# Ten units' bonus products and a weight subtraction moved from GpSimd to VectorE, a weight addition and a range check moved in the order

## The chip, the cores and the metric

The kernel runs on one core of one Trainium2 chip. The metric is device time in microseconds (us). Engines are named as in the profile: PE (TensorE), PEld (its weight loads), DVE (VectorE), ACT (ScalarE), POOL (GpSimd), SP (SyncE, which issues the DMAs).

## The reference

Three stages follow each other, in float32. B, H, S, D = 4, 8, 768, 48; d_model 384; d_ff 1024; 4 experts of width 64.

```python
for t in range(S):                                     # 1: a linear recurrence, per batch and head
    cur = k_t (x) v_t                                  # outer product, D x D
    y_t = r_t @ (state + u * cur)
    state = w_t[:, None] * state + cur
h = relu(x @ w_in)                                     # 2: gated MLP with a convolution of 3 taps along S
c = conv3(h, conv_w)
x = (h * sigmoid(c)) @ w_out
out = sum over the 2 chosen of 4 experts of gate_e * (causal_softmax_attention_e(x) @ wo_e)   # 3
```

## The kernel before

Stages 1 and 2 run interleaved in `phase1`, in an order written out by hand for PE, DVE, ACT and POOL: what `slot(u)` calls, call by call, is what each engine does in that order. SP's DMAs are ordered by a scheduler. Stage 3 (class `Attention`) follows and is not touched.

Stage 1 is cut into 32 units (a batch, a half of the sequence, a pair of heads). `slot(u)` finishes unit u, prepares unit u+1 and does the output of unit u-1. For unit u+1 it runs, on DVE, `scan_d` (Dp, a running product, L205), `scan_f` (L210, Fp L212, K L215) and `queries` (Q, L220); on POOL `bonus` (L225, L226: r times k, times u, 128x288, in place); then `diag`: DVE sums the bonus to e (L231), and POOL spreads e onto a diagonal tile AT with two affine_selects (L234). For unit u it runs `check` (two ACT passes over w, L243, a range test that feeds a flag), and on PE `trans` (L266) and its ACT copy KT, `scores` (L252), `state` (L278); on DVE `carry` (L289 reads the state product from PSUM, L292 twice chains it over the chunks) and `masked` (L258, two copy_predicated that put the scores from PSUM into AT). For unit u-1, `yout` (PE L306, L312) and `rows` (ACT L324, DVE L325, a small POOL cast, and DMAs into X).

PSUM tiles of `trans`, `state` and `yout` come from one pool of two buffers ("m"), used in turn. So `trans(u+1)` takes the buffer that `state(u)` wrote, and waits until `carry(u)` has read it in L289.

Stage 2 starts in slot 5 with two groups a slot (`groups`): `mlp1` (PE L350, nine matmuls into hs, one PSUM buffer; ACT ht L354, ct L358), `conv` (DVE, two scalar_tensor_tensor, L369/L371 or L373/L374, then ACT tanh L377), `gate` (DVE L387), `mlp2` (PE L400, four groups later).

The weights w_in and w_out arrive as float64 in eight pieces of 768 numbers a partition and are turned to float32 by hand, two buffers each for the raw piece and the work tiles: `load_w` (DMA), `conv1_w` (ACT L72; DVE L75 and L76; POOL L77, an integer addition), and, for w_in alone, `conv2_w` (ACT L173 rounds to the high part, POOL L174 subtracts it for the low part). `check_w` (ACT L185, L186) tests a piece that is loaded a second time for values outside the range. The table `WS` says in which slot a piece is taken. `conv_w` converts the 24 convolution weights.

Of the kernel before, what the change touches and what calls it, by code (L numbers as in the profile page):

```python
# [16 lines left out]
OP = mybir.AluOpType  # L17
# [3 lines left out]
B, H, S, D = 4, 8, 768, 48  # L21
# [8 lines left out]
CH = NC // 2  # L30
# [10 lines left out]

X2_ON_DVE, V_ON_DVE, OUT_ON_DVE = (), (1,), (5,)
SCALED_ON_POOL = 13


def _f(ap):
    return ap.bitcast(F32)
# [40 lines left out]
def phase1(tc, nc, a, x2, ident, stat, lim, top, right, left2):  # L88
# [15 lines left out]
    T = {}  # L104
# [55 lines left out]
    def conv1_w(n, i):  # L160

        if wide:
            RW[n, i] = f64_fast(nc, raw, RW[n, i], WC, "w", None if n == "win" else wl(wout)[:, i * WC:(i + 1) * WC])

    def conv2_w(n, i):

        t = RW.pop((n, i))
        if n == "wout":
            if not wide:
                nc.scalar.activation(wl(wout)[:, i * WC:(i + 1) * WC], t, AF.Copy)  # L170
            return
        d0, d1 = (wl(d)[:, i * WC:(i + 1) * WC] for d in win)
        nc.scalar.activation(d0, t, AF.Copy)  # L173
        nc.gpsimd.tensor_tensor(d1, t, _f(d0), op=OP.subtract)  # L174

    RW = {}

    def check_w(n, i):

        if not wide:  # L180
            return
        t = RW.pop((n, i))
        o = 4 * NU + (i if n == "win" else 4 + i)
        hi = t.bitcast(F32).rearrange("p (n two) -> p n two", two=2)[:, :, 1]
        nc.scalar.activation(hi, hi, AF.Square)  # L185
        nc.scalar.activation(hi, hi, AF.Relu, bias=lim[:, 3:4], scale=-1.0, accum_out=stat[:, o:o + 1])  # L186
# [35 lines left out]
    def bonus(u):  # L222
        b, h, hp = split(u)
        m = T[u]["rn"]
        nc.gpsimd.tensor_tensor(m, m, T[u]["kn"], op=OP.mult)  # L225
        nc.gpsimd.tensor_tensor(m, m, u_b[:, hp][:, :, None].to_broadcast([128, 2, CH, D]), op=OP.mult)  # L226

    def diag(u):
        t = T[u]
        e = wk.tile([128, 2, CH], F32, name="e")  # L230
        nc.vector.tensor_reduce(e, t["rn"], axis=AX.X, op=OP.add)  # L231
        AT = t["AT"] = wk.tile([128, 2, CH, C], F32, name="AT")
        for j in range(2):
            nc.gpsimd.affine_select(AT[:, j], e[:, j][:, :, None].to_broadcast([128, CH, C]),  # L234
                                    pattern=[[0, CH], [1, C]], compare_op=OP.is_equal, fill=0.0, base=0,
                                    channel_multiplier=-1)

    def check(u):
        t = T[u]
        w, Fp = t["w"], t["Fp"]  # L240
        wc = w[:, 1:].rearrange("p (c t) -> p c t", c=CH)[:, :, 0:C]
        for z in range(2):
            nc.scalar.activation(Fp[:, :, 0:C], wc, AF.Relu, bias=lim[:, z:z + 1], scale=(-1.0, 1.0)[z],  # L243
                                 accum_out=stat[:, 2 * u + z:2 * u + z + 1])
# [135 lines left out]
    def gate(g):  # L380
        if not 0 <= g < NG:
            return
        h = g // NF % 2
        o, N = 2 * h, HT - 2 + 4 * h
        ht, st = G[g]
        gt = ml.tile([128, HT + 2], F32, name="gt", bufs=6)[:, 0:N]
        nc.vector.scalar_tensor_tensor(gt, st, 1.0, ht[:, o:o + N], op0=OP.add, op1=OP.mult)  # L387
        G[g] = gt
# [3 lines left out]
    def mlp2(g):  # L392
# [9 lines left out]
        if f == NF - 1:  # L402
# [11 lines left out]
    mine = mybir.EngineType  # L414
    mine = {mine.PE, mine.DVE, mine.Activation, mine.Pool}

    WS = ((2, "win", 0), (3, "win", 1), (4, "win", 2), (5, "wout", 0), (6, "win", 3), (7, "wout", 1), (8, "wout", 2),
          (9, "wout", 3)) + tuple((10 + i, ("win", "wout")[i % 2], i // 2) for i in range(8))

    def groups(g, last=False):  # L420
        if 0 <= g < NG:
            mlp1(g)
        if 0 <= g - LAG < NG:
            mlp2(g - LAG)

    def slot(u):

        ga = 2 * u - G0
        s1u, nxt = u < 2 * NU, u + 1 < 2 * NU
        for i, (z, n, m) in enumerate(WS):  # L430
            if u == z - 2:
                load_w(n, m)
        if s1u:
            trans(u)
        conv(ga - 1)
        if nxt:
            bonus(u + 1)
            scan_d(u + 1)
        for i, (z, n, m) in enumerate(WS[0:8]):
            if u == z:  # L440
                conv1_w(n, m)
        gate(ga - 1)
        groups(ga)
        if nxt:
            scan_f(u + 1)
        conv(ga)
        if nxt:
            queries(u + 1)
        gate(ga)
        if s1u:  # L450
            check(u)
            scores(u)
            state(u)
        if 0 < u <= 2 * NU:
            yout(u - 1)
        if nxt:
            diag(u + 1)
        if s1u:
            carry(u)
            masked(u)  # L460
        if 0 < u <= 2 * NU:
            rows(u - 1)
        for i, (z, n, m) in enumerate(WS):
            if u == z:
                (conv2_w if i < 8 else check_w)(n, m)
        if u == 1:
            conv_w()
        if u == 18:
            rawc.close()
        groups(ga + 1)  # L470
        if u + 3 < 2 * NU:
            load(u + 3)
# [646 lines left out]
```

## Time and profile before

| | |
|---|---|
| time, median of 3 runs | 658.96 us (657.47 to 659.04) |
| the profiled execution | 659.13 us, span of its trace 657.4 us |
| PE / DVE / ACT / POOL busy | 586.6 / 517.6 / 347.9 / 183.2 us |
| mean granted TensorE clock | 0.962 |

The span is the time from the first to the last instruction; the 1.7 us between it and the profiled execution's own time lie around it. Busy time is an average over stages; which engine sets the pace differs from stage to stage.

### The profile page before, as it was taken

Reading aid. Unit: us, or ns where it says so; the run is one execution under the profiler, and the core shown is the slowest. Engines: PE = TensorE matmul, PEld = TensorE weight load, DVE = VectorE, ACT = ScalarE, POOL = GpSimd, SP = SyncE. Lnnn points to the kernel's source line nnn. Section 1 sums busy time; section 2 is a strip of 40 time slices with the busy share of each in tenths; the row PEclk is TensorE's granted clock in tenths of the full one; section 3 lists DMA queues with packets and bytes.
Section 4 is the critical chain, followed back from the end, with each engine's and each line's share of the span. In section 5 each row is a group of like instructions: output and inputs, shape, how many; then the busy total and the mean of one; then the engine's idle time right before and its main releaser. Section 6 shows DMA issues by size and latency. Waiting matters only on the chain.

```text
span 657.4 us, 11247 instructions
## 1 busy us (share of the span) xinstructions
PE 586.6 (89%) x3978; PEld 464.9 (71%) x3978; DVE 517.6 (79%) x1151; ACT 347.9 (53%) x819; POOL 183.2 (28%) x245
## 2 busy tenths in 40 slices
PE   2665689799999999999999999989997999799896
PEld 1553567577676777777777776968786987788754
DVE  6999999988888999999995643688765876776471
ACT  3233444566666545556355552666654665556452
POOL 6478444222222233224321710030002002102260
PEclk9957789989999999999999999999998999999999
DMA  8655445475774455454513652265036514442502
GB/s 315 214 162 208 171 151 178 147 230 179 219 215 135 126 165 158 133 169 134 160 59 96 173 139 67 85 170 144 25 90 175 145 37 128 126 98 84 133 1 77
DMA packets 34401, 92.39 MB, mean 141 GB/s; under 512 B 5024, under 2 KB 14368, under 8 KB 34336
## 3 DMA queue, kind: packets, MB, share of 16 engines
q1 hardware_dynamic: 34336, 91.59, 46.7%
q8 instruction: 33, 0.54, 0.3%
q14 instruction: 32, 0.26, 0.1%
HBM read 53.77 MB, written 9.44 MB: 96 GB/s over the span
## 4 chain that ended last, share of the span: by engine, by line
PE 48%; DVE 29%; ACT 9%; DMA 7%; issue 4%; SPq 2%; POOL 1%; ACTq 0%; DVEq 0%; POOLq 0%
PE x L400 9%; PE hs L350 7%; PE m L767 6%; PE st L841 5%; PE m L891 5%; PE t L875 4%; DVE Fp L212 4%; PE m L903 4%; PE m L797 3%; DVE Dp L205 3%; DMA x<-x 2%; DVE AT L258 2%; DVE wm L76 2%; DVE ct L374 2%; DVE ct L369 2%
## 5 line engine op out<-in xcount | busy, mean ns | idle before, releaser
L400 PE MATMUL x<-gt,wout 128*128 128x386 f32 (+1 forms) x384 | 135.0, 490 | 0.0
L350 PE MATMUL hs<-X,win 128*128 128x384 f32 (+1 forms) x576 | 121.7, 357 | 8.2 <-ACT ht L354 8.1
L350 PEld LDWEIGHTS hs<-X,win 128*128 128x128 f32 x576 | 101.1, 193 | 17.6 <-ACT ht L354 11.7
L377 ACT ACTIVATE st<-ct 128x382 f32<-128x382 f32 (+1 forms) x64 | 33.6, 525 | 126.3 <-DVE ct L371 67.4
L400 PEld LDWEIGHTS x<-gt,wout 128*128 128x128 f32 x384 | 73.0, 192 | 35.8 <-issue 1.2
L855 ACT ACTIVATE A<-sm,mn 128x128 f32<-128x128 f32 (+5 forms) x96 | 63.8, 665 | 28.3 <-DVE mn L854 27.5
L854 DVE CUSTOM_DVE_ANT_0 sm<-st,mask 128x128 f32<-128x128 f32 (+5 forms) x96 | 58.3, 619 | 20.8 <-PE st L841 18.2
L234 POOL TENSOR_SCALAR_AFFINE_SELECT AT<-e 128x384 f32<-128x384 f32 x64 | 32.4, 531 | 141.8 <-DVE e L231 134.2
L875 PE MATMUL t<-ident,A 128*128 128x128 f32 x336 | 53.5, 276 | 2.1 <-ACT T L879 1.2
L266 PE MATMUL m<-ident,K 128*128 128x128 f32 x80 | 16.6, 312 | 36.6 <-DVE Ss L289 26.4
L841 PE MATMUL st<-sk,sq 128*128 128x384 f32 (+3 forms) x128 | 44.8, 360 | 2.7 <-DVE mn L854 1.8
L753 POOL TENSOR_TENSOR xs<-x,xs 128x768 fp32r<-128x768 f32 x12 | 22.4, 1884 | 88.8 <-ACT xs L752 88.8
L881 DVE COPY T<-t 128x128 f32<-128x128 f32 (+3 forms) x64 | 32.2, 504 | 18.4 <-PE t L875 17.9
L387 DVE SCALAR_TENSOR_TENSOR gt<-st,ht 128x382 f32<-128x382 f32 (+1 forms) x64 | 38.1, 596 | 10.9 <-ACT st L377 7.9
L841 PE MATMUL st<-sl,sq 128*128 128x384 f32 (+3 forms) x128 | 41.1, 334 | 5.8 <-DMA sl<-kl 5.8
L875 PEld LDWEIGHTS t<-ident,A 128*128 128x128 f32 x336 | 40.3, 140 | 8.4 <-issue 2.2
L252 PEld LDWEIGHTS sc<-Q,K 64*128 64x128 f32 x384 | 30.7, 218 | 20.5 <-issue 5.6
L266 PEld LDWEIGHTS m<-ident,K 128*128 128x128 f32 x80 | 11.0, 156 | 46.8 <-DVE Ss L289 29.8
L891 PE MATMUL m<-T,V 128*64 128x384 f32 (+2 forms) x288 | 43.8, 422 | 0.0
L879 ACT ACTIVATE T<-t 128x512 f32<-128x512 f32 (+3 forms) x64 | 28.6, 447 | 25.4 <-PE t L875 20.6
L252 PE MATMUL sc<-Q,K 64*128 64x128 f32 x384 | 37.6, 325 | 4.2 <-DVE AT L258 4.2
L358 ACT ACTIVATE ct<-ht,cwk 128x382 f32<-128x382 f32 (+1 forms) x64 | 39.5, 617 | 2.0
(126 smaller groups left out, 1216.2 us busy)
## 6 DMA issues: line engine op xcount, KB each, us to landing
wkr<-in_wkr SPq DMA_DIRECT2D x32, 578.0 KB, 3.8
rkv<-in_rkv SPq DMA_DIRECT2D x32, 480.0 KB, 4.5
rawt<-in_win SPq DMA_DIRECT2D x8, 768.0 KB, 5.5
rawt<-in_wout SPq DMA_DIRECT2D x8, 768.0 KB, 5.2
sk<-kh SPq DMA_DIRECT2D x32, 192.0 KB, 3.3
sl<-kl SPq DMA_DIRECT2D x32, 192.0 KB, 4.0
x<-x SPq DMA_DIRECT2D x12, 384.0 KB, 3.9
out_dram<-ot SPq DMA_DIRECT2D x24, 192.0 KB, 1.9
```

The lines of the kernel that those rows point to most:

```text
L252: nc.tensor.matmul(sc[j][:, c], t["K"][p, c], t["Q"][p, c], start=True, stop=True)
L350: nc.tensor.matmul(hs[:, 0:N], win[wi][:, f // 2, i, (f % 2) * 128:(f % 2 + 1) * 128], x[:, i, xi], start=(n == 0), stop=(n == 8))
L358: nc.scalar.activation(ct, ht[:, o:o + N], AF.Copy, scale=w[:, 1, f:f + 1])
L377: nc.scalar.activation(st, ct, AF.Tanh)
L387: nc.vector.scalar_tensor_tensor(gt, st, 1.0, ht[:, o:o + N], op0=OP.add, op1=OP.mult)
L400: nc.tensor.matmul(acc[0][i][:, 0:N], wout[:, f, i * 128:(i + 1) * 128], gt, start=(f == 0), stop=(f == NF - 1))
L767: nc.tensor.matmul(pt[:, 0:HT], w[wi][:, i, p * 128:(p + 1) * 128], xs[xi][:, i, s], start=(m == 0), stop=(m == 8))
L841: nc.tensor.matmul(st[:, z, 0:n], q[:, qi * C:(qi + 1) * C], k[:, z * n:(z + 1) * n], start=(i == 0), stop=(i == 1))
L854: nc.vector.tensor_tensor_reduce(o3, i3, m3, 1.0, 3e38, op0=OP.add, op1=OP.min, accum_out=mn)
L855: nc.scalar.activation(at, o3, AF.Exp, bias=mn, scale=-1.0, accum_out=rs[:, qi % 3:qi % 3 + 1])
L875: nc.tensor.transpose(pt[:, ki - k0], at[:, ki * C:(ki + 1) * C], self.ident)
L891: nc.tensor.matmul(po[o, lo:HT], V[:, ki, (2 * p + j) * 64:(2 * p + j + 1) * 64], Ts[j][:, ki, lo:], start=(ki == 0), stop=(ki == n - 1))
```

## The change

- `bonus` runs on DVE for units 0 to 9 and stays on POOL for the others. On DVE it is called right before `diag`, behind `yout` in the code, and no longer at the slot's start.
- `conv2_w`'s subtraction runs on DVE. It is now called early in the slot after the one in which the piece was added; `conv1_w` is now called late in the slot, between `diag` and `masked`, one slot number earlier.
- `masked` and `rows` now come ahead of `carry` on DVE.
- `check` is called ahead of `conv(ga)`, and `check_w` ahead of `scores`; in ACT's order the first is now ahead of the second tanh, the second ahead of `rows`' copy.
- `conv_w` moves from slot 1 to slot 0. The second loads for `check_w` are issued a slot later.

```diff
+BONUS_ON_DVE = 10
...
         d0, d1 = (wl(d)[:, i * WC:(i + 1) * WC] for d in win)
         nc.scalar.activation(d0, t, AF.Copy)
-        nc.gpsimd.tensor_tensor(d1, t, _f(d0), op=OP.subtract)
+        nc.vector.tensor_tensor(d1, t, _f(d0), op=OP.subtract)
...
         m = T[u]["rn"]
-        nc.gpsimd.tensor_tensor(m, m, T[u]["kn"], op=OP.mult)
-        nc.gpsimd.tensor_tensor(m, m, u_b[:, hp][:, :, None].to_broadcast([128, 2, CH, D]), op=OP.mult)
+        eng = nc.vector if u < BONUS_ON_DVE else nc.gpsimd
+        eng.tensor_tensor(m, m, T[u]["kn"], op=OP.mult)
+        eng.tensor_tensor(m, m, u_b[:, hp][:, :, None].to_broadcast([128, 2, CH, D]), op=OP.mult)
...
-    WS = ((2, "win", 0), (3, "win", 1), (4, "win", 2), (5, "wout", 0), (6, "win", 3), (7, "wout", 1), (8, "wout", 2),
-          (9, "wout", 3)) + tuple((10 + i, ("win", "wout")[i % 2], i // 2) for i in range(8))
+    WS = ((1, "win", 0), (2, "win", 1), (3, "win", 2), (4, "wout", 0), (5, "win", 3), (6, "wout", 1), (7, "wout", 2),
+          (8, "wout", 3))
+    WC2 = tuple((10 + i, ("win", "wout")[i % 2], i // 2) for i in range(8))
...
-            if u == z - 2:
+        for z, n, m in WS + WC2:
+            if u == z - 1:
                 load_w(n, m)
...
-            bonus(u + 1)
+            if u + 1 >= BONUS_ON_DVE:
+                bonus(u + 1)
             scan_d(u + 1)
-        for i, (z, n, m) in enumerate(WS[0:8]):
-            if u == z:
-                conv1_w(n, m)
+        for z, n, m in WS:
+            if u == z + 1:
+                conv2_w(n, m)
         gate(ga - 1)
         groups(ga)
+        if s1u:
+            check(u)
...
         gate(ga)
+        for z, n, m in WC2:
+            if u == z:
+                check_w(n, m)
         if s1u:
-            check(u)
             scores(u)
             state(u)
...
         if nxt:
+            if u + 1 < BONUS_ON_DVE:
+                bonus(u + 1)
             diag(u + 1)
+        for z, n, m in WS:
+            if u == z:
+                conv1_w(n, m)
         if s1u:
-            carry(u)
             masked(u)
         if 0 < u <= 2 * NU:
             rows(u - 1)
-        for i, (z, n, m) in enumerate(WS):
-            if u == z:
-                (conv2_w if i < 8 else check_w)(n, m)
-        if u == 1:
+        if s1u:
+            carry(u)
+        if u == 0:
             conv_w()
```

In the orders below the changed kernel's lines stand up to 11 numbers higher than those named so far. First, DVE at the program's start, before:

```order
L205 SCALAR_TENSOR_TENSOR Dp<-wkr,cD 128x387
L141 CAST msk<-Q 128x384
L210 RECIPROCAL cF<-Dp 128x3
L212 SCALAR_TENSOR_TENSOR Fp<-wkr,cF 128x387
L215 TENSOR_TENSOR K<-wkr,Fp 128x384
L220 TENSOR_TENSOR Q<-wkr,Dp 128x384
L231 TENSOR_REDUCE e<-rkv 128x6
```

and now:

```order
L142 CAST msk<-Q 128x384
L227 TENSOR_TENSOR rkv<-rkv 128x288
L228 TENSOR_TENSOR rkv<-rkv,u_b 128x288
L206 SCALAR_TENSOR_TENSOR Dp<-wkr,cD 128x387
L211 RECIPROCAL cF<-Dp 128x3
```

The first unit's bonus, which reads u_b, now stands ahead of the first scan. Second, DVE in slot 3 (unit 4 prepared, a piece of w_in in work as wm, Y of unit 2), before:

```order
L205 SCALAR_TENSOR_TENSOR Dp<-wkr,cD 128x387
L75 TENSOR_SCALAR wm<-rawt 128x768
L76 SCALAR_TENSOR_TENSOR wm<-rawt,wm 128x768
L210 RECIPROCAL cF<-Dp 128x3
L212 SCALAR_TENSOR_TENSOR Fp<-wkr,cF 128x387
L215 TENSOR_TENSOR K<-wkr,Fp 128x384
L220 TENSOR_TENSOR Q<-wkr,Dp 128x384
L231 TENSOR_REDUCE e<-rkv 128x6
L289 TENSOR_TENSOR Ss_128<-m,Dp 128x3x48
L292 SCALAR_TENSOR_TENSOR Ss_128<-Ss_128,Dp 128x48 x2
L258 COPY_PREDICATED AT<-msk,sc 128x384 x2
L325 TENSOR_TENSOR Y<-m,Y 128x384
```

and now, from Q on into the next slot's start:

```order
L221 TENSOR_TENSOR Q<-wkr,Dp 128x384
L227 TENSOR_TENSOR rkv<-rkv 128x288
L228 TENSOR_TENSOR rkv<-rkv,u_b 128x288
L233 TENSOR_REDUCE e<-rkv 128x6
L76 TENSOR_SCALAR wm<-rawt 128x768
L77 SCALAR_TENSOR_TENSOR wm<-rawt,wm 128x768
L260 COPY_PREDICATED AT<-msk,sc 128x384 x2
L327 TENSOR_TENSOR Y<-m,Y 128x384
L291 TENSOR_TENSOR Ss_128<-m,Dp 128x3x48
L294 SCALAR_TENSOR_TENSOR Ss_128<-Ss_128,Dp 128x48 x2
L206 SCALAR_TENSOR_TENSOR Dp<-wkr,cD 128x387
L175 TENSOR_TENSOR win_139<-wm,win_138 128x768
```

The two weight steps that POOL's addition (now L78) waits for stand ahead of the three operations that read PSUM (AT, Y, the first of Ss), and the reading of the state product (now L291) is the third of these. Third, ACT in slot 12, where a piece is checked (rawt), before:

```order
L377 ACTIVATE st<-ct 128x386
L354 ACTIVATE ht<-hs 128x388
L358 ACTIVATE ct<-ht,cwk 128x386
L377 ACTIVATE st<-ct 128x386
L243 ACTIVATE Fp,stat<-wkr,lim 128x3x128 x2
L324 ACTIVATE Y<-m 128x384
L185 ACTIVATE rawt<-rawt 128x768
L186 ACTIVATE rawt,stat<-rawt,lim 128x768
L354 ACTIVATE ht<-hs 128x388
```

and now:

```order
L379 ACTIVATE st<-ct 128x386
L356 ACTIVATE ht<-hs 128x388
L360 ACTIVATE ct<-ht,cwk 128x386
L245 ACTIVATE Fp,stat<-wkr,lim 128x3x128 x2
L379 ACTIVATE st<-ct 128x386
L186 ACTIVATE rawt<-rawt 128x768
L187 ACTIVATE rawt,stat<-rawt,lim 128x768
L326 ACTIVATE Y<-m 128x384
L356 ACTIVATE ht<-hs 128x388
```

The unit's check went ahead of the second tanh, and the piece's check from behind Y to ahead of it.

## Rows read from the trace of the kernel before

**Rows 1.** Stretches: from:to and length in us, busy us (x instructions) by engine, TensorE clock, DMA
```profile
25.33:122.27 96.94, 66.41 (x477) 51.34 (x476) 94.73 (x140) 39.03 (x85) 53.60 (x53) 0.79 0.55 179
122.27:211.71 89.44, 84.08 (x611) 63.30 (x610) 76.93 (x145) 58.42 (x126) 22.88 (x41) 0.98 0.64 193
211.71:334.63 122.92, 122.71 (x916) 93.35 (x915) 119.02 (x218) 64.88 (x153) 38.70 (x60) 1.00 0.46 143
```

**Rows 2.** Groups of instructions, DVE, 25.33 to 122.27: busy us, mean ns
```profile
L212 DVE TENSOR_TENSOR_SCAN Fp<-wkr,cF 128x387 f32<-128x387 f32 x8 | 14.6, 1822 | 0.3
L76 DVE SCALAR_TENSOR_TENSOR wm<-rawt,wm 128x768 int32<-128x768 int32 x8 | 12.2, 1519 | 0.3
L220 DVE TENSOR_TENSOR Q<-wkr,Dp 128x384 f32<-128x384 f32 x8 | 9.2, 1150 | 0.0
L215 DVE TENSOR_TENSOR K<-wkr,Fp 128x384 f32<-128x384 f32 x8 | 7.1, 890 | 0.3
L369 DVE SCALAR_TENSOR_TENSOR ct<-ht,cwk,ct 128x381 f32<-128x381 f32 x8 | 6.2, 769 | 0.0
```

**Rows 3.** Single lines, DVE, whole span: ns min/median/max, first and last start
```profile
L212 DVE TENSOR_TENSOR_SCAN Fp<-wkr,cF x32: 964/965/2412, 6.0 to 336.2; 128x387 f32<-128x387 f32 x32
L76 DVE SCALAR_TENSOR_TENSOR wm<-rawt,wm x8: 957/959/2458, 27.4 to 110.8; 128x768 int32<-128x768 int32 x8
L220 DVE TENSOR_TENSOR Q<-wkr,Dp x32: 546/553/2153, 8.0 to 338.8; 128x384 f32<-128x384 f32 x32
L215 DVE TENSOR_TENSOR K<-wkr,Fp x32: 557/559/1977, 7.5 to 337.2; 128x384 f32<-128x384 f32 x32
L369 DVE SCALAR_TENSOR_TENSOR ct<-ht,cwk,ct x32: 600/616/1269, 68.5 to 364.4; 128x381 f32<-128x381 f32 x32
L205 DVE TENSOR_TENSOR_SCAN Dp<-wkr,cD x32: 946/958/1568, 4.7 to 334.6; 128x387 f32<-128x387 f32 x32
L75 DVE TENSOR_SCALAR wm<-rawt x8: 527/529/535, 26.8 to 110.3; 128x768 int32<-128x768 int32 x8
L292 DVE SCALAR_TENSOR_TENSOR Ss<-Ss,Dp x64: 269/436/456, 14.9 to 348.7; 128x48 f32<-128x48 f32 x64
```

**Rows 4.** Timeline, DVE and POOL, slot 3: start us, us, instruction
```profile
41.00 2.15 DVE L220 TENSOR_TENSOR Q<-wkr,Dp 128x384 f32<-128x384 f32 x1
...
40.62 2.11 POOL L77 TENSOR_TENSOR wm<-wm,wy 128x768 int32<-128x768 int32 x1
```

**Rows 5.** Timeline, POOL, slot 22
```profile
259.92 0.80 POOL L225 TENSOR_TENSOR rkv<-rkv 128x288 f32<-128x288 f32 x1
260.80 0.81 POOL L226 TENSOR_TENSOR rkv<-rkv,u_b 128x288 f32<-128x288 f32 x1
```

**Rows 6.** Timeline, DVE, slot 22
```profile
258.67 0.25 DVE L289 TENSOR_TENSOR Ss<-m,Dp 128x96 f32<-128x96 f32 x1
...
259.80 1.06 DVE L258 COPY_PREDICATED AT<-msk,sc 128x384 f32<-128x384 uint32 x2
260.75 0.54 DVE L325 TENSOR_TENSOR Y<-m,Y 128x384 fp32r<-128x384 f32 x1
```

**Rows 7.** Timeline, the start, POOL and DVE; in brackets the idle time ahead
```profile
8.37 0.79 POOL L226 TENSOR_TENSOR rkv<-rkv,u_b 128x288 f32<-128x288 f32 x1 [1.74 <-DMA u_b<-in_u]
...
9.20 0.45 DVE L231 TENSOR_REDUCE e<-rkv 128x6 f32<-128x288 f32 x1 [0.69 <-POOL rkv L226]
```

**Rows 8.** Timeline, ACT, slot 17, in which a piece is checked
```profile
206.58 0.47 ACT L324 ACTIVATE Y<-m 128x384 fp32r<-128x384 f32 x1
206.95 0.91 ACT L185 ACTIVATE rawt<-rawt 128x768 f32<-128x768 f32 x1
...
208.90 0.47 ACT L354 ACTIVATE ht<-hs 128x388 f32<-128x388 f32 x1
```

**Rows 9.** Who waited for whom, 122.27 to 211.71: us in total, times, longest
```profile
DVE ct L369 <- ACT ct L358: 4.9, 4, 1.2
```

**Rows 10.** Timeline, PE, slot 22
```profile
260.36 0.38 PE L266 MATMUL m<-ident,K 128*128 128x128 f32 x2
```

More of the change, by code (lines that the diff above doesn't have):

```diff
@@ L462, in slot @@
             rows(u - 1)
-        for i, (z, n, m) in enumerate(WS):
-            if u == z:
-                (conv2_w if i < 8 else check_w)(n, m)
-        if u == 1:
+        if s1u:
+            carry(u)
+        if u == 0:
             conv_w()
```

## The prediction

> **What bounds the kernel now.** I read the busy time by stretches first, cutting stages 1 and 2 at the starts of the Dp scans, since one Dp runs in each slot. Three regimes show [rows 1]. From 25.33 to 122.27 us (slots 2 to 9) DVE is busy 94.73 of 96.94 us and PE 66.41: DVE sets the pace. From 211.71 to 334.63 (slots 18 to 29) PE is busy 122.71 of 122.92, so a slot lasts 122.92 / 12 = 10.24 us whatever DVE does. Between them (slots 10 to 17, those in which a weight piece is checked) PE is busy 84.08 of 89.44 us, so 5.36 us is the most that can be had there. After 334.63 nothing in the change matters but its shift in time.
>
> Next I asked what DVE's busy time is made of. The reader should set the mean of a line in slots 2 to 9 [rows 2] against its median over the span [rows 3]: the scan Fp takes 1.822 us where 0.965 is usual, L76 1.519 for 0.959, Q 1.150 for 0.553, K 0.890 for 0.559, the first convolution operation 0.769 for 0.616. Nothing in these operations changed; they are held. The timeline says by whom: Q starts at 41.00 and needs 2.15 us, while POOL's 768-wide addition runs from 40.62 to 42.73 [rows 4]; Q ends 0.42 us after it. So DVE operations with two SBUF inputs wait for POOL, and count as busy. This is also what tells which operations are immune: in slot 22 POOL's two products run from 259.92 to 261.61 [rows 5], and copy_predicated twice in 1.06 us and Y in 0.54 us, which read PSUM, are not stretched beside them [rows 6].
>
> **Slots 2 to 9, what goes.** Per line, eight times the difference: Fp 6.9, L76 4.5, Q 4.8, K 2.6, the convolution 1.2; Dp reaches 1.568 instead of 0.958 [rows 3] in two of these slots, 1.2 more. Sum 21.2 us of holding by the bonus products, the weight additions and the subtractions. The two carry operations of a slot take 0.436 each by the median and 0.269 at best [rows 3], since POOL's affine_selects run beside them; in the new order those run beside other work: 16 x 0.167 = 2.7 us. One slot's weight steps, 0.53 + 0.96 = 1.5 us, leave for slot 1. Together 25.4 us go.
>
> **Slots 2 to 9, what comes.** Four subtractions of 768 elements on DVE: no row has one there, L76 has the same two-input shape, 0.96 each, 3.8 us. Seven units' bonus on DVE, two products of 288 elements: between the 288-element sum of 0.45 [rows 7] and the 384-element product of 0.55 [rows 3], so 0.47, nearest the first; 14 x 0.47 = 6.6 us (bounds 6.3 to 7.7). And a new holding. The addition now starts behind L76 and takes 2.1 us [rows 4]; DVE has copy_predicated (0.95 from start to start), Y (0.46) and the first carry operation (0.3) to run beside it [rows 6], 1.7 us, and then the two carry operations have to wait. Ahead of that, L76 meets the affine_selects. Bounds for one slot: 0.45 us (2.1 less 1.7, and nothing for the affine_selects) to 2.1 us (the whole addition, no cover at all). I take 1.0, near the lower end, because rows 5 and 6 show the cover at work: 0.4 for L76 (two of the 0.167 above, rounded up) and 0.6 for the carry, the addition starting some 0.2 us late behind the second affine_select. Seven slots: 7.0 us. Together 17.4 come. Net: **-8.0 us**.
>
> [...]
>
> **The start and slots 0 and 1.** DVE now begins with the first unit's bonus, whose second product waits for u_b: POOL started it at 8.37 us after waiting 1.74 for that DMA [rows 7]. Dp, Fp, K and Q of the first unit, done before e at 9.20 until now [rows 7], queue behind it: 8.37 + 0.47 + 0.96 + 0.2 + 0.97 + 0.56 + 0.55, less 0.3 for the overlap of neighbours, gives e at about 11.8: +2.6 us, and nothing covers it, since DVE is the bound. In slots 0 and 1 holding by four bonus products goes (some 0.5 each, at most the 0.61 of Dp) and 4 x 0.167 of the carry, 2.7 in all; two bonus pairs (1.9), slot 1's weight steps (1.5) and its new holding (1.0) come: +1.7. The work on the 24 convolution weights moves a slot and stays as long. Net **+4.3 us**.
>
> **Slots 10 to 17, the checks.** ACT now runs a piece's check behind Y and ahead of the next ht: from 206.95 to 208.90, 1.95 us [rows 8]. DVE waits for the following ct 4.9 us in four slots [rows 9] and as long again for the other half's (the same row with L373), 1.2 a slot. In the new order the check stands between the second tanh and Y. Then ht comes in time, but Y comes later: from the end of the convolution ACT needs 0.5 (tanh) + 1.95 + 0.47 [rows 8] = 2.9 us to Y's end, DVE has Q, gate, e and copy_predicated, 2.4 us, so it waits 0.5. Out 9.8, in 4.0: 5.8, more than PE's 5.36. I take 3.4, because POOL's products of the next unit, which run behind Y, now meet the two carry operations instead of DVE's wait, some 0.3 us a slot. Bounds 0 and 5.4: **-3.4 us**. The second loads of the pieces, a slot later on SP's queue, still have about a slot to land.
>
> **Slots 18 to 29.** PE is the bound, 0.2 us idle in all. The DVE time saved there (0.33 a slot) buys nothing: **0**. What could be lost there is the second rival.
>
> **Sum.** 4.3 - 8.0 - 3.4 = -7.1 us. Against the profiled execution's 659.13 us (span 657.4 and 1.7 around it, neither changed otherwise) that is **652.0 us**. The profiled execution lies 0.2 us above the median of the runs, 658.96, within their spread.
>
> **The rivals.**
> 1. *More is gained.* The new holding is only 0.45 us a slot (8 x 0.55 = 4.4 less, slot 1 included) and the checks reach PE's floor (2.0 less): 645.6 us. For it: PSUM readers are plainly immune [rows 5, 6]. Against: two affine_selects stand between e and the addition.
> 2. *PE waits for the carry: slower.* `trans(u+1)` needs the PSUM buffer that L289 reads, and L289 moves behind copy_predicated and Y, 1.4 us. In slot 22 it ends at 258.92 [rows 6] and PE starts trans at 260.36 [rows 10]: 1.44 us of slack, all of it used up. Where slack is less, PE, which is the bound, waits; at half of 1.4 us in each of the 20 slots from 10 to 29 that is 14 us, and the checks' 3.4 are lost too: 669.4 us. It decides once DVE's slot is no shorter than PE's 10.24. Against: DVE is busy 119.02 / 12 = 9.9 us a slot [rows 1], 0.33 less in the new order, so it runs ahead until the slack is back.
> 3. *The holding only moves.* L75 and the affine_selects fight as well, the addition starts later and outlasts the PSUM readers by more: 1.8 us a slot, 8 x 0.8 = 6.4 more: 658.4 us, no change. [...]
>    That the change doesn't do what it says can be left out: the orders show it.
>
> **How the numbers follow.** Forecast 0.52 (its own range 648 to 656), more gained 0.20, holding moves 0.15, PE waits 0.13. About 0.3%, 2 us, is what a measurement of this kernel can tell from no change: 657.0 to 661.0. Faster: all of the first two and a third of the third case, 0.77; the same 0.10; slower 0.13. The range from 644 to 658 leaves out the second rival and half of the third, 0.2.
>
> **What would show it.** Right: e of the first unit starts near 11.8 us instead of 9.20; in slots 2 to 8 Fp, K and Q stand at 0.97, 0.56 and 0.55 us; the operations that are still long are the two-input weight step and the carry pair; DVE's wait for ct in slots 10 to 17 is gone and a short one ahead of Y takes its place. Wrong: trans on PE waits for the carry in slots 18 to 29 (rival 2), or the carry pair takes over 1.5 us (rival 3).

## The result and the profile after

The changed kernel takes 649.31 us (median of 4 runs, 647.54 to 651.82) against 659.0 us before: ratio 0.9859, 95% interval 0.9821 to 0.9897. In a second comparison it took 650.25 against 662.38 us, ratio 0.9808 (0.9771 to 0.9846). So it is faster by 1.4 to 1.9%; the forecast was 652.0 us. The profiled execution took 649.97 us, with a span of 648.2 us.

The busy time of the changed kernel by the stretches of [rows 1], cut at the Dp scans of the same units (the first line is the time from the first Dp to unit 3's, the last one what follows unit 31's); columns as there:

```profile
8.15:28.17 20.02, 10.47 (x79) 8.06 (x79) 18.65 (x42) 5.26 (x15) 7.44 (x9) 0.95 0.71 267
28.17:115.30 87.13, 62.45 (x494) 49.16 (x495) 83.50 (x156) 40.10 (x86) 30.96 (x35) 0.80 0.62 198
115.30:200.81 85.51, 83.60 (x615) 61.95 (x614) 79.44 (x146) 58.87 (x126) 26.55 (x41) 1.00 0.62 200
200.81:322.21 121.40, 121.40 (x913) 92.58 (x912) 117.38 (x218) 67.13 (x153) 38.43 (x60) 1.00 0.48 147
322.21:648.20 325.99, 304.64 (x1884) 249.59 (x1882) 208.87 (x619) 178.91 (x438) 53.56 (x56) 0.98 0.38 101
```

Set beside [rows 1], each stretch has its entry in the sum:

| stretch | before | after | difference | forecast |
|---|---|---|---|---|
| start, slots 0 and 1 | 25.33 | 28.17 | +2.84 | +4.3 |
| slots 2 to 9 | 96.94 | 87.13 | -9.81 | -8.0 |
| slots 10 to 17 | 89.44 | 85.51 | -3.93 | -3.4 |
| slots 18 to 29 | 122.92 | 121.40 | -1.52 | 0 |
| the rest | 322.77 | 325.99 | +3.22 | 0 |
| span | 657.4 | 648.2 | -9.20 | -7.1 |

The last two lines need care. The cuts are DVE's; in slots 18 to 29 PE sets the pace and DVE's place beside it shifts. By the start of a unit's K transposes on PE (L266 before, L268 after) the lead over the kernel before is 10.63 us at unit 18, 11.54 at units 23 to 30 and 11.84 at unit 31. So PE was ahead by nearly 12 us when stage 1 ended, and in this pair of executions stage 3, which the change does not touch, gave 2.6 us back. Both halves are followed up below.

The groups of DVE instructions in slots 2 to 9 (busy us, mean ns, idle ahead), to be set beside [rows 2]:

```profile
L77 DVE SCALAR_TENSOR_TENSOR wm<-rawt,wm 128x768 int32<-128x768 int32 x7 | 8.1, 1156 | 0.2
L213 DVE TENSOR_TENSOR_SCAN Fp<-wkr,cF 128x387 f32<-128x387 f32 x8 | 7.7, 964 | 0.3
L294 DVE SCALAR_TENSOR_TENSOR Ss<-Ss,Dp 128x48 f32<-128x48 f32 x17 | 7.7, 453 | 0.6
...
L371 DVE SCALAR_TENSOR_TENSOR ct<-ht,cwk,ct 128x381 f32<-128x381 f32 x8 | 4.9, 610 | 0.0
L216 DVE TENSOR_TENSOR K<-wkr,Fp 128x384 f32<-128x384 f32 x8 | 4.5, 558 | 0.3
L221 DVE TENSOR_TENSOR Q<-wkr,Dp 128x384 f32<-128x384 f32 x8 | 4.4, 551 | 0.0
...
L175 DVE TENSOR_TENSOR win<-wm,win 128x768 fp32r<-128x768 f32 x4 | 3.8, 959 | 0.9 <-ACT win L174 0.9
...
L228 DVE TENSOR_TENSOR rkv<-rkv,u_b 128x288 f32<-128x288 f32 x7 | 3.2, 458 | 0.2
```

Fp, K, Q and the convolution stand at their free values, 0.964, 0.558, 0.551 and 0.610 us, as forecast: nothing holds them any more. What is still long is the two-input weight step L77 (1.156 for 0.959) and L294.

Slot 3 of the changed kernel on DVE and POOL (start us, us, instruction) shows the new cover:

```profile
43.51 0.55 DVE L76 TENSOR_SCALAR wm<-rawt 128x768 int32<-128x768 int32 x1
43.73 1.90 POOL L236 TENSOR_SCALAR_AFFINE_SELECT AT<-e 128x384 f32<-128x384 f32 x2 [5.94 <-DVE e L233]
...
44.09 1.16 DVE L77 SCALAR_TENSOR_TENSOR wm<-rawt,wm 128x768 int32<-128x768 int32 x1
...
45.17 1.05 DVE L260 COPY_PREDICATED AT<-msk,sc 128x384 f32<-128x384 uint32 x2
...
45.60 1.81 POOL L78 TENSOR_TENSOR wm<-wm,wy 128x768 int32<-128x768 int32 x1
46.11 0.54 DVE L327 TENSOR_TENSOR Y<-m,Y 128x384 fp32r<-128x384 f32 x1
46.57 0.29 DVE L291 TENSOR_TENSOR Ss<-m,Dp 128x144 f32<-128x144 f32 x1
...
46.90 0.88 DVE L294 SCALAR_TENSOR_TENSOR Ss<-Ss,Dp 128x48 f32<-128x48 f32 x2
```

The addition runs from 45.60 to 47.41. DVE's three operations that read PSUM lie beside it at full speed (1.05, 0.54, 0.29 us); only the carry pair, 0.57 us where nothing runs beside it, takes 0.88 and ends 0.37 us after the addition. Ahead of that L77 and the affine_selects share the time: L77 is 0.2 us longer, the two affine_selects take 1.90 us.

### The profile page after: what moved, and what is told of

The parts are those of the page before. It is cut to its first block, busy times and chain, and to the rows that moved or that the text cites. A ratio compares the mean times of both kernels' runs of the same rounds, so it can differ in the third digit from the quotient of the medians.

```text
span 648.2 us, 11247 instructions
## 1 busy us (share of the span) xinstructions
PE 582.6 (90%) x3978; PEld 461.3 (71%) x3978; DVE 509.0 (79%) x1175; ACT 351.8 (54%) x819; POOL 160.7 (25%) x221
## 4 chain that ended last, share of the span: by engine, by line
PE 57%; DVE 21%; DMA 9%; ACT 6%; issue 3%; SPq 2%; POOL 1%; ACTq 0%; DVEq 0%; POOLq 0%
PE x L402 11%; PE hs L352 10%; PE m L778 6%; PE st L852 5%; PE m L902 5%; PE t L886 4%; PE m L914 4%; PE m L808 3%; PE sc L254 3%; DMA x<-x 2%; DVE Fp L213 2%; PE m L308 2%; DMA rkv<-in_rkv 2%; DMA wkr<-in_wkr 2%; PE m L314 2%
## 5 line engine op out<-in xcount | busy, mean ns | idle before, releaser
L402 PE MATMUL x<-gt,wout 128*128 128x386 f32 (+1 forms) x384 | 133.5, 485 | 0.0
L352 PE MATMUL hs<-X,win 128*128 128x384 f32 (+1 forms) x576 | 119.2, 352 | 0.6 <-DMA X<-Y 0.4
L352 PEld LDWEIGHTS hs<-X,win 128*128 128x128 f32 x576 | 99.5, 190 | 6.8 <-issue 4.1
L236 POOL TENSOR_SCALAR_AFFINE_SELECT AT<-e 128x384 f32<-128x384 f32 x64 | 40.5, 657 | 182.9 <-DVE e L233 170.5
L268 PE MATMUL m<-ident,K 128*128 128x128 f32 x80 | 17.2, 320 | 42.3 <-DVE Y L327 30.9
L268 PEld LDWEIGHTS m<-ident,K 128*128 128x128 f32 x80 | 10.1, 156 | 55.7 <-DVE Y L327 41.2
L389 DVE SCALAR_TENSOR_TENSOR gt<-st,ht 128x382 f32<-128x382 f32 (+1 forms) x64 | 40.8, 637 | 10.5 <-ACT st L379 7.4
L270 ACT ACTIVATE KT<-m 128x384 f32<-128x384 f32 (+1 forms) x32 | 14.0, 438 | 54.7 <-PE m L268 54.4
L356 ACT ACTIVATE ht<-hs 128x384 f32<-128x384 f32 (+1 forms) x64 | 31.0, 484 | 22.0 <-PE hs L352 21.8
L254 PEld LDWEIGHTS sc<-Q,K 64*128 64x128 f32 x384 | 28.7, 216 | 17.2 <-issue 15.1
```

Of the source, the lines that this page charges most:

```text
L254: nc.tensor.matmul(sc[j][:, c], t["K"][p, c], t["Q"][p, c], start=True, stop=True)
L352: nc.tensor.matmul(hs[:, 0:N], win[wi][:, f // 2, i, (f % 2) * 128:(f % 2 + 1) * 128], x[:, i, xi], start=(n == 0), stop=(n == 8))
L402: nc.tensor.matmul(acc[0][i][:, 0:N], wout[:, f, i * 128:(i + 1) * 128], gt, start=(f == 0), stop=(f == NF - 1))
```

## The experiments

Each kernel's trace was read at the same four points: how much later (+) or earlier (-) than in the kernel before PE starts the K transposes of units 3, 10, 18 and 31. This takes stages 1 and 2 apart from what stage 3 does. Times are medians, ratios are to the kernel before on the same chip.

| kernel | unit 3 | unit 10 | unit 18 | unit 31 | time, us | ratio (interval) |
|---|---|---|---|---|---|---|
| changed | +4.40 | -5.35 | -10.63 | -11.84 | 649.31 | 0.9859 (0.9821 to 0.9897) |
| changed, second time | +4.69 | -5.09 | -10.65 | -12.02 | 650.25 | 0.9808 (0.9771 to 0.9846) |
| all bonus on GpSimd | +2.95 | -7.38 | -12.11 | -13.34 | 648.33 | 0.9779 (0.9715 to 0.9844) |
| subtraction on GpSimd | +5.46 | -3.27 | -8.11 | -9.40 | 651.14 | 0.9825 (0.9761 to 0.9890) |
| checks in the old place | +4.58 | -5.17 | -7.76 | -8.60 | 653.72 | 0.9855 (0.9788 to 0.9921) |
| carry first | +4.97 | +1.80 | -3.81 | -3.48 | 657.78 | 0.9929 (0.9900 to 0.9959) |
| addition beside the scans | +6.77 | +2.51 | -3.83 | -5.19 | 655.48 | 0.9899 (0.9866 to 0.9932) |
| first bonus on GpSimd | +2.68 | -7.09 | -11.95 | -12.98 | 646.81 | 0.9766 (0.9723 to 0.9809) |
| checks alone | +0.35 | +0.12 | -5.31 | -5.02 | 654.87 | 0.9896 (0.9854 to 0.9939) |
| changed, third x buffer | +4.95 | -4.84 | -9.95 | -10.97 | 644.25 | 0.9764 (0.9723 to 0.9804) |
| before, third x buffer | +0.31 | +0.40 | -0.51 | 0.00 | 656.31 | 0.9949 (0.9923 to 0.9975) |
| first bonus and third buffer | +2.64 | -7.13 | -11.55 | -12.65 | 643.20 | 0.9739 (0.9695 to 0.9782) |

Two traces of the changed kernel agree within 0.3 us at each point. A part of every number is the start, which the edits do not explain: u_b's product begins when its DMA has landed, at 7.77 us in the first trace of the changed kernel and at 7.96 to 8.49 us in the six others that begin as it does, and the first unit's transposes come 3.28 us later in each, at 11.05 and at 11.24 to 11.78 us. From unit 3 to unit 10 the five traces whose code is the same there agree within 0.04 us (75.99 to 76.03 us), so differences between two points say more than the number at one.

### Is it the bonus? All bonus products on GpSimd

```diff
-BONUS_ON_DVE = 10
+BONUS_ON_DVE = 0
```

> The changed kernel with all 32 units' bonus products back on GpSimd at the slot's start; all else as changed. Theory (a product of 0.8 us on GpSimd holds VectorE by 0.4 to 0.6, about what it costs VectorE itself, 0.47): slots 1 to 8 within 2 us of the changed kernel's in all, and the wait for u_b at the start is gone, 2 us less: 645 to 649 us. Rival (taking the bonus off GpSimd is what gave the gain): slots 1 to 8 longer by 0.8 us each or more, 655 us or above.

Unit 10 starts 2.0 us earlier than in the changed kernel, 1.45 of them already there at unit 3. From unit 3 to unit 10 this kernel gains 10.33 us, the changed one 9.75. The 2.0 us are won at the start: the first unit's transposes come 2.43 us earlier (8.62 for 11.05 us), and from there to unit 10 this kernel takes 0.4 us longer. The groups of DVE in slots 2 to 9 of this kernel show why ten units' products on DVE buy next to nothing:

```profile
L294 DVE SCALAR_TENSOR_TENSOR Ss<-Ss,Dp 128x48 f32<-128x48 f32 x17 | 11.0, 648 | 0.6
...
L175 DVE TENSOR_TENSOR win<-wm,win 128x768 fp32r<-128x768 f32 x4 | 5.4, 1352 | 0.4 <-ACT win L174 0.4
```

The products on POOL hold L294 (11.0 us for 7.7), L175 (5.4 for 3.8) and a little of Fp, K, the convolution and the gate; on DVE they cost 6.4 us of their own (L227 and L228, 3.2 each). In this order it comes to nearly the same.

### Does the subtraction pay on DVE?

```diff
-        nc.vector.tensor_tensor(d1, t, _f(d0), op=OP.subtract)
+        nc.gpsimd.tensor_tensor(d1, t, _f(d0), op=OP.subtract)
```

> The changed kernel with the four subtractions back on GpSimd. Theory: each takes about 1.9 us there and holds Fp or the scan beside it by about 1.4 us, against 0.96 us as an instruction of VectorE's own: 0.4 to 0.6 us more in each of four slots, 650.5 to 652 us. Rival (GpSimd's work costs nothing where VectorE goes on beside it): 4 x 0.96 less, 645.5 us.

Unit 10 starts 2.1 us later, but 0.7 us of this is the start (11.78 for 11.05 us). Slots 2 to 9 take 88.57 us for 87.13, 1.4 more. Four subtractions beside Fp and K, from the groups of DVE in these slots:

```profile
L213 DVE TENSOR_TENSOR_SCAN Fp<-wkr,cF 128x387 f32<-128x387 f32 x8 | 10.7, 1340 | 0.3
...
L216 DVE TENSOR_TENSOR K<-wkr,Fp 128x384 f32<-128x384 f32 x8 | 7.3, 918 | 0.3
```

Fp costs 3.0 us more, K 2.8; L175's 3.8 us on DVE are saved, and so are the 0.9 us in which it waited for ACT. Net 1.1 of the 1.4 us.

### Does the place of the addition matter? Two ways to take its cover away

First the carry ahead of the operations that read PSUM:

```diff
         if s1u:
+            carry(u)
             masked(u)
         if 0 < u <= 2 * NU:
             rows(u - 1)
-        if s1u:
-            carry(u)
```

> The changed kernel with carry ahead of masked and rows again, still behind the weight steps. Theory (the addition must run beside the three operations that read PSUM): the two carry operations wait for nearly the whole addition, 1.3 to 1.5 us a slot in place of 0.3 to 0.5, in slots 1 to 8: 656 to 659 us; slots 18 to 29 unchanged. Rival (PE's wait for the carry is what counts): PE's trans comes earlier and the kernel is as fast or up to 3 us faster, 646 to 649 us.

Slot 3 of this kernel, DVE and POOL:

```profile
48.02 1.99 DVE L294 SCALAR_TENSOR_TENSOR Ss<-Ss,Dp 128x48 f32<-128x48 f32 x2
...
48.12 1.83 POOL L78 TENSOR_TENSOR wm<-wm,wy 128x768 int32<-128x768 int32 x1
49.94 1.04 DVE L260 COPY_PREDICATED AT<-msk,sc 128x384 f32<-128x384 uint32 x2
```

The carry pair now meets the addition at once and stands through it: 1.99 us for 0.57. Unit 10 starts 7.15 us later than in the changed kernel: 0.7 us of this is the start, 6.6 us come between units 3 and 10, about 0.9 us for each of the seven weight slots there.

Then the addition itself beside Fp and K, all else as in the changed kernel:

```diff
         for z, n, m in WS:
+            if u == z:
+                conv1_w(n, m)
+        for z, n, m in WS:
             if u == z + 1:
                 conv2_w(n, m)
...
-        for z, n, m in WS:
-            if u == z:
-                conv1_w(n, m)
```

> The changed kernel with one step of a weight slot moved: the piece's first step (ScalarE's rounding, L76, L77 and GpSimd's addition) stands right behind the Dp scan, ahead of the other piece's second step, so that the addition runs beside Fp and K, which read two SBUF tiles, and no longer beside copy_predicated and Y. Theory (where the addition stands is what gave the gain of slots 2 to 9: PSUM readers are not held, two-input SBUF operations are): Fp or K is held about 1.4 us in each of the eight weight slots instead of the 0.5 us of the changed kernel, so about 0.9 us a slot, 7 us in all by unit 10's transposes, 655 to 657 us; Fp's mean goes from 0.96 to over 1.5. Rival (the gain came from the bonus leaving these slots and from L175 alone, the place of the addition does not matter): unit 10's transposes start within 1.5 us of the changed kernel, 649 to 651 us.

Slot 3 of this kernel, and the group of Fp in slots 2 to 9:

```profile
42.58 2.36 POOL L78 TENSOR_TENSOR wm<-wm,wy 128x768 int32<-128x768 int32 x1 [3.07 <-DVE wm L77]
...
43.40 2.37 DVE L213 TENSOR_TENSOR_SCAN Fp<-wkr,cF 128x387 f32<-128x387 f32 x1
...
48.30 0.99 POOL L236 TENSOR_SCALAR_AFFINE_SELECT AT<-e 128x384 f32<-128x384 f32 x2 [3.37 <-DVE e L233]
```

```profile
L213 DVE TENSOR_TENSOR_SCAN Fp<-wkr,cF 128x387 f32<-128x387 f32 x8 | 14.7, 1842 | 0.3
```

Fp stands at 1.842 us again, as in the kernel before (1.822 [rows 2]), and unit 10 starts 7.9 us later than in the changed kernel, 0.6 us of it from the start. In slots 2 to 9 (91.79 us for 87.13) Fp's eight runs cost 7.0 us more, K and the gate 3.0; L77, the carry pair and L175's wait, which nothing lengthens now, give back 4.9. The affine_selects, now beside copy_predicated, take 0.99 us for both; in the changed kernel they took 1.90. With the start set aside, the two ways of losing the cover cost 6.5 and 7.3 us by unit 10: that the addition stands beside PSUM readers is most of what slots 2 to 9 gained by. The subtraction adds 1.4 us, the bonus about 0.4.

### What are the checks worth? Undone, and done alone

In the changed kernel `check` and `check_w` go back to their old places:

```diff
-        if s1u:
-            check(u)
         if nxt:
             scan_f(u + 1)
...
-        for z, n, m in WC2:
-            if u == z:
-                check_w(n, m)
         if s1u:
+            check(u)
             scores(u)
             state(u)
...
         if s1u:
             carry(u)
+        for z, n, m in WC2:
+            if u == z:
+                check_w(n, m)
```

> The changed kernel with both range checks back in their old places in ScalarE's order (the unit's check behind the second gate, the piece's check behind Y). Theory (the piece's check ahead of ht kept PE waiting): PE's idle time of some 5 us in slots 10 to 17 comes back, 653.5 to 655 us, and slots 18 to 29 do not change. Rival (those slots gained from the order on VectorE, not from the checks): at most 1 us more, 650 us.

Up to unit 10 nothing differs (-5.17 for -5.35, the start); from there to unit 18 the gain is 2.6 us instead of 5.3, and 3.2 us are missing at unit 31. The waits of slots 10 to 17 in this kernel (us in total, times, longest):

```profile
DVE ct L371 <- ACT ct L360: 4.9, 4, 1.6
...
PE hs L352 <- ACT ht L356: 4.5, 8, 1.2
```

DVE's wait for ct is back with its 4.9 us for one half [rows 9] and 2.6 us for the other (L375). PE waits 4.5 us for ht; in the kernel before it was 5.4, in the changed one there is no such wait, but 1.9 us for Y. The expectation of some 5 us was too high: the rest of the change takes 2.6 us from these slots without the checks.

The other way round, the kernel before with the new order of the checks only:

```diff
+        if s1u:
+            check(u)
         if nxt:
             scan_f(u + 1)
...
+        for i, (z, n, m) in enumerate(WS):
+            if u == z and i >= 8:
+                check_w(n, m)
         if s1u:
-            check(u)
             scores(u)
...
-            if u == z:
-                (conv2_w if i < 8 else check_w)(n, m)
+            if u == z and i < 8:
+                conv2_w(n, m)
```

> The kernel before with only ScalarE's order of the checks changed (check_d of the unit ahead of scan_f, the weight piece's check between the second gate and the scores); bonus, subtractions, additions and carry as before. Theory (ct late for DVE is a loss of its own, independent of the rest): slots up to 9 stay as before within 1 us, units 10 to 18 gain 3 to 5.4 us, most of PE's idle time there, 654 to 656 us. Rival (the checks pay only because the carry and the first steps moved too, without them DVE's slot is the bound): under 2 us gained by unit 18, 657 to 659 us.

Unit 10 starts at +0.12 and unit 18 at -5.31: 5.4 us from ACT's order alone. That is as much as PE's idle time in [rows 1], 5.36 us, but it is not that idle time. These slots in the kernel with the checks alone, columns as in [rows 1]:

```profile
122.50:206.00 83.50, 81.62 (x610) 61.85 (x610) 80.83 (x145) 58.89 (x128) 25.75 (x41) 1.00 0.64 206
```

PE is still idle for 1.88 us. The rest of the gain is PE's own work, which is shorter. In slot 10 of the kernel before, PE (in brackets its idle time ahead) and a window over it:

```profile
131.76 2.75 PE L350 MATMUL hs<-X,win 128*128 128x388 f32 x9 [2.05 <-ACT ht L354]
```

```profile
130.00:135.00 5.00, 3.24 (x11) 2.94 (x12) 3.76 (x7) 3.47 (x8) 1.75 (x3) 0.74 0.83 228
```

Behind this wait of 2.05 us the granted clock falls: it is 0.57 from 132 to 136 us, and the nine matmuls take 2.75 us where those of the group before took 1.87. The trace of the kernel before with a third x buffer, further down, has the same wait of 2.05 us, and the nine matmuls behind it take 3.19 us. In the eleven other traces PE waits for ht 1.20 us at the most in these slots and no group of nine takes over 1.88 us; the mean clock over them is 1.00 in the changed kernel, with the checks in the old place and with the checks alone. Cut at PE's own transposes of units 10 and 18, the kernel before takes 90.27 us with PE busy for 84.86, the checks alone 84.84 with 82.96, the changed kernel 84.99 with 83.08. So ACT's order took 3.5 us of waiting and 1.9 us of a lower clock, and 1.9 us of waiting are left both ways. Alone the checks give 5.4 us, on top of the rest 2.7: without them, in the changed kernel's other order, the mean clock of these slots is 1.00 as well. Gains that do away with the same wait don't add.

### The start: the first unit's bonus back on GpSimd

```diff
-        eng = nc.vector if u < BONUS_ON_DVE else nc.gpsimd
+        eng = nc.vector if 0 < u < BONUS_ON_DVE else nc.gpsimd
```

> The changed kernel with the bonus of the first unit alone back on GpSimd. Theory (the first term of the prediction: DVE's wait for u_b at the start and the four operations queued behind it are a plain loss): e of the first unit starts at 9.2 to 9.6 us instead of 11.29, every later milestone comes 2.0 to 2.4 us earlier, 647 us. Rival (the start is covered by loads that come later, or Fp and K are held by the products on GpSimd by as much): unit 3's transposes start within 0.5 us of the changed kernel's, 649 to 650 us.

The start in the changed kernel, DVE:

```profile
7.77 0.46 DVE L228 TENSOR_TENSOR rkv<-rkv,u_b 128x288 f32<-128x288 f32 x1 [1.32 <-DMA u_b<-in_u]
8.15 0.96 DVE L206 TENSOR_TENSOR_SCAN Dp<-wkr,cD 128x387 f32<-128x387 f32 x1
...
11.29 0.45 DVE L233 TENSOR_REDUCE e<-rkv 128x6 f32<-128x288 f32 x1
```

and with this product on POOL:

```profile
8.38 1.16 POOL L228 TENSOR_TENSOR rkv<-rkv,u_b 128x288 f32<-128x288 f32 x1 [1.37 <-DMA u_b<-in_u]
9.58 0.45 DVE L233 TENSOR_REDUCE e<-rkv 128x6 f32<-128x288 f32 x1 [0.69 <-POOL rkv L228]
```

Dp, Fp, K and Q run while POOL waits for u_b; e starts 1.7 us earlier, and PE's milestones come 1.7 us earlier at units 3 and 10, a little less than expected, and 1.1 at unit 31. u_b came 0.6 us later here (8.38 for 7.77 us); set beside the changed kernel with a third x buffer, further down, where u_b's product began at 8.35, units 3 and 10 come some 2.3 us earlier. The time is 646.81 us for 650.25 on the same chip, 3.4 us less; what stage 3 adds to this was not followed. The wait at the head was a plain loss.

### What stage 3 gives back

The changed kernel was run once more on the chip of the last three:

> The changed kernel once more, on the chip of these three, as the measure for them. 647.5 to 652 us; the gain stands at 10.5 to 12 us by unit 23's transposes, and what is left of it at the end (9 to 10 us) depends on whether the granted clock falls in stage 3, which the runs so far show at different places.

The lead of about 12 us at unit 31 came again, and the profile lost 3.5 us of it by the end of the span, set against the one profiled execution of the kernel before. By the medians of this second comparison nothing is lost, 662.38 - 650.25 = 12.1 us: there the kernel before had spans of 658.6 to 663.2 us, all longer than its profiled 657.4. So what follows explains that pair of profiles; how much stage 3 gives back on average is not shown. PE in the middle of stage 3, the kernel before (in brackets the idle time ahead and its releaser):

```profile
560.90 0.50 PE L841 MATMUL st<-sl,sq 128*128 128x256 f32 x2 [0.92 <-DMA sl<-kl]
...
565.50 0.61 PE L767 MATMUL m<-xs,wq 128*128 128x384 f32 x2 [1.70 <-ACT xs L752]
...
567.77 0.50 PE L841 MATMUL st<-sk,sq 128*128 128x512 f32 x1 [1.07 <-DVE mn L854]
...
569.91 0.34 PE L841 MATMUL st<-sl,sq 128*128 128x384 f32 x1
```

and the changed kernel at the same place (xs is ACT's copy of x, which the products with wq read):

```profile
549.01 0.51 PE L852 MATMUL st<-sl,sq 128*128 128x256 f32 x2 [0.27 <-DMA sl<-kl]
...
554.50 0.61 PE L778 MATMUL m<-xs,wq 128*128 128x384 f32 x2 [2.59 <-ACT xs L763]
...
556.77 0.80 PE L852 MATMUL st<-sk,sq 128*128 128x512 f32 x1 [0.86 <-DVE mn L865]
...
560.67 0.52 PE L852 MATMUL st<-sl,sq 128*128 128x384 f32 x1
```

The lead is 11.89 us at the first pair, 11.00 at the second (the wait for xs is 0.89 longer), 9.24 at the last. In that last piece PE's matmuls are slower: the 128x512 one takes 0.80 us for 0.50. The windows say why. Before:

```profile
560.00:565.00 5.00, 2.90 (x19) 2.63 (x19) 2.37 (x10) 1.60 (x6) 0.00 (x0) 1.00 0.66 194
565.00:570.00 5.00, 3.43 (x19) 3.02 (x20) 3.62 (x14) 3.95 (x13) 1.83 (x1) 1.00 0.00 0
```

after:

```profile
550.00:555.00 5.00, 2.41 (x18) 2.13 (x17) 1.45 (x7) 2.38 (x8) 0.47 (x1) 1.00 0.46 145
555.00:560.00 5.00, 4.14 (x15) 3.43 (x14) 4.10 (x14) 3.13 (x11) 1.36 (x1) 0.53 0.00 0
```

Behind the longer idle time the granted clock (the column ahead of the last two) is 0.53; before it stayed at 1.00. That is 1.8 us, with the longer wait 2.65, as much as the span lost. The changed kernel's second trace and three experiments show the same: a wait for xs of 2.30 us, of 2.28 (subtraction on GpSimd), 2.54 (checks in the old place) and 2.46 (first bonus on GpSimd), and a mean clock of 0.91 to 0.96 from 540 to 580 us. With the carry first and with the addition beside the scans the mean clock is 0.96 over the same time; with the checks alone the wait is 1.54 us and the clock stays at 1.00, as in the kernel before. It does not go by the lead: at unit 31 the kernel with the checks alone was 5.02 us ahead, and the one with the addition beside the scans, whose clock is 0.79 from 560 to 565 us, 5.19. Why the wait is longer in one than in the other is not shown.

xs waits for the third of a batch's three x loads, which stands behind eight key copies and two outputs on SP's queue because there are two x buffers. So three were tried, in the changed kernel, in the kernel before, and with the first unit's bonus on GpSimd:

```diff
-            x = xp.tile([128, S], F32, name="x", bufs=2)
+            x = xp.tile([128, S], F32, name="x", bufs=3)
```

> The changed kernel with three buffers instead of two for the x tiles that stage 3 loads, so that the third load of a batch no longer stands on SP's queue behind the key copies and outputs. Theory (stage 3 gives back 2.7 us of what slots 0 to 17 won, because PE waits 2.59 us for that third load and the granted clock then stands at 0.50 for some five us): the wait ahead of L778 in the middle of stage 3 goes, the clock stays at 1.00 between 550 and 565 us, 4 to 5 us less than the changed kernel, 645 to 646 us. Rival (the loads that follow come later by as much, or the clock falls at the next idle stretch): 648 to 651 us.

> The kernel before with the same third buffer. Theory: it has a wait of 1.70 us there and no fall of the clock in its trace, so it gains 1 to 2 us only: 657 to 658 us against 659 to 660; with this buffer in both, the change is worth what slots 0 to 17 show, 11 to 12 us. Rival (the buffer is worth the same to both, and the clock's fall is not what separates them): 654 to 656 us.

> The changed kernel with the first unit's bonus on GpSimd and with the third buffer: the two gains have nothing to do with each other, so 1.5 to 2.4 us under the run with the buffer alone, 643 to 644.5 us. Rival: no better than the first unit's bonus alone, 646 to 647 us.

The times are 644.25, 656.31 and 643.20 us. The first lies 0.75 us under its range, the third in its own, though 1.05 us under the first and not 1.5 or more. The reason given does not hold: the clock still falls, only at another place. The changed kernel with three buffers:

```profile
540.00:545.00 5.00, 2.29 (x9) 0.95 (x9) 3.56 (x5) 0.60 (x1) 1.79 (x1) 0.59 0.86 223
545.00:550.00 5.00, 5.00 (x29) 4.36 (x26) 1.62 (x6) 1.65 (x5) 0.00 (x0) 0.73 0.00 0
```

and the kernel before with three, shifted by 10 us:

```profile
550.00:555.00 5.00, 2.29 (x11) 1.25 (x13) 4.18 (x5) 0.60 (x1) 2.41 (x2) 0.71 0.93 227
555.00:560.00 5.00, 5.00 (x26) 3.97 (x23) 0.98 (x2) 1.09 (x2) 0.00 (x0) 0.60 0.07 24
```

The earlier loads move an idle time of 2.7 us, with a fall behind it, in front of the xs matmuls in both kernels; the wait for xs is gone. The kernel before gained 3.5 us instead of the 1 to 2 expected, between theory and rival. Where both kernels have this fall, the change is worth 656.31 - 644.25 = 12.1 us; the lead at unit 31 in their traces is 10.97. The pair with two buffers differed by 12.1 us as well in the second comparison, so it is not shown that the fall is what separates the two. When the clock falls was not settled. The wait's length alone doesn't say it: with all bonus on GpSimd PE waited only 1.45 us for xs, less than the 1.70 of the kernel before, and the clock fell to 0.50; that trace has other idle time close by. The best kernel of all is the last of the table, 643.20 us.

## Why the prediction was right, and where its terms were off

**Direction and bound: right.** DVE set the pace in slots 2 to 9, PE in 18 to 29, as read from [rows 1]; the sign of every term came true. The forecast of 652.0 is 2.7 us above the median, nearer than its terms deserve: three of them were too cautious, in the profile by 4.7 us in all at unit 31, and a loss that no term held hid over half of that. That the two errors have opposite signs is luck; by the medians of the second comparison, 12.1 us, the sum of 7.1 is 5 us short.

- **The start and slots 0 and 1: +4.3, measured +2.84.** The queueing behind u_b is shown by the first-bonus run. The head was e at 11.8, measured 11.29 for 9.20, since u_b's product began at 7.77 and not at 8.37; in the six other traces with this start e begins at 11.48 to 12.02, so this part was right within the scatter. The mis-sized part is the rest, 0.75 us instead of 1.7.
- **Slots 2 to 9: -8.0, measured -9.81.** What goes was right line by line, since the free values came. The four subtractions cost their 0.96 us each, and 0.9 us in all of waiting for ACT; the bonus cost 6.4 for 6.6. The mis-sized term is the new holding, 1.0 us a slot: L77 gives 0.2 and the carry, over seven weight slots, 17 x (0.453 - 0.269) / 7 = 0.45. Together 0.65, near the lower bound of 0.45. The affine_selects were counted as holding DVE by 0.4; they lose more themselves, 0.9 us.
- **L77 beside the affine_selects.** The 0.4 us a slot for it was an estimate from the carry's 0.167; slot 3 shows 0.2. Read one by one there, the first affine_select runs from 43.73 to 44.44, and L77, begun at 44.09, is 0.2 us longer: only 0.35 us of the affine_select were left. The second, begun at 44.39, takes 1.24 us where the shortest takes 0.52, and ends at 45.63, 0.38 us after L77. So each time the one that began later was the longer one. With the long addition, in the carry-first kernel, the carry pair, begun at 48.02 and 0.10 us ahead of the addition, took 1.99 us for 0.57 and ended 0.06 us after it.
- **Slots 10 to 17: -3.4, measured -3.93 by DVE and -5.28 by PE's transposes.** DVE's wait for ct is gone and a short one ahead of Y came. The waits of these slots in the changed kernel:

```profile
DVE Y L327 <- ACT Y L326: 3.4, 8, 0.4
PE m L268 <- DVE Y L327: 1.9, 7, 0.4
```

  It is 0.4 a slot where 0.5 was forecast. PE's idle time falls from 5.36 to 1.91 us, 3.45 where 3.4 was forecast, but that is near for another reason than the one given for taking 2 us off: POOL's products do hold the carry pair, yet what PE still waits for is Y. And 5.36 us was not the most that could be had: in the kernel before the granted clock fell once in these slots, and without that fall PE's own work is 1.8 us shorter. No term held this.
- **Slots 18 to 29: 0.** PE has no idle time there at all (121.40 of 121.40); the 0.9 us that its lead grows from unit 18 to 23 was not traced further. Rival 2 fails: no transpose waits for the carry. Rival 3 fails: no run shows its 1.8 us of holding a slot; the carry pair takes 0.88 to 1.07 us in slots 2 to 7 and 1.49 in slot 8, where POOL's next bonus product runs beside it, not over 1.5, and L76, which it feared for, 0.55 for 0.53. Beside POOL's bonus products, in slots 10 to 17, the pair does reach 1.77.
- **Rival 1, more gained,** is nearest to what slots 1 to 17 did: 0.65 us of holding a slot, and 5.28 us in slots 10 to 17, of which 1.8 are the clock. By its 645.6 us the kernel should be 3.7 us faster than it is. The term that failed there and in the forecast alike is "after 334.63 nothing in the change matters but its shift in time": the profiled execution lost 2.6 us of its lead to a longer wait for a DMA and a lower clock behind it, and the size of the shift does not say when that happens. The lead at unit 31 was 11.84 us for a sum of 7.1, 4.7 more than forecast, and the loss takes 2.6 of these.

## What to carry to other kernels

In these traces GpSimd's addition (1.8 us) cost VectorE nothing beside operations that read PSUM (1.05, 0.54 and 0.29 us), and 1.4 us beside one with two SBUF inputs (Fp 2.37 us for 0.96, the carry pair 1.99 for 0.57); so look for three or four short PSUM readers in a slot and order them behind whatever starts the long GpSimd instruction. Before moving small products to VectorE, compare what they hold where they are with what they cost as VectorE's own work: here the two were nearly equal, and the one product that waits for a late load should not stand at the head of the engine that bounds. Gains that do away with the same wait don't add (the checks: 5.4 us alone, 2.7 on top of the rest), in the kernel before a wait of PE of 2.05 us was followed by four us at a clock of 0.57, another 1.8 us, and a lead won early has to be followed through the untouched stages before it is counted.

## What the runs showed of the hardware that was not expected

- Beside L76 and L77, in slot 3 of the changed kernel, the two affine_selects took 1.90 us instead of 0.99, while L76 stayed at 0.55 and L77 went from 0.96 to 1.16: the one that came while the other was under way lost, and POOL came behind twice.
- In the kernel before the granted clock was 0.57 over four us behind one wait of 2.05 us in slot 10; nine matmuls of 1.87 us took 2.75, and 3.19 behind the same wait in the kernel before with a third x buffer. With the checks alone PE waits 2.14 us for unit 10's transposes, and the nine matmuls behind them take 1.86 us; from 122.5 us on the mean clock is 1.00.
- In the middle of stage 3 the granted clock was 0.50 from 556 to 562 us in the changed kernel, behind a wait for xs of 2.59 us, and 0.50 from 555 to 560 us with all bonus on GpSimd, behind one of 1.45; in the same place, behind 1.70 us (the kernel before) and 1.54 (the checks alone), it stayed at 1.00. A matmul of 0.50 us took 0.80 in the changed kernel's fall.
